# Attention in rounds of two pairs, with one PSUM ring of four bank pairs

## The chip, the core and the metric

The kernel runs on one core of a Trainium2 chip. The metric is the device time of one execution, in microseconds (us); the median of three runs is compared. All times below come from the runs of the kernel before and from one profiled execution of it.

## What is computed

Sigmoid attention over 8 batches of 12 heads (448 positions, head width 64), whose output, laid out as 3584 tokens by 768, goes through a feed-forward network with leaky ReLU:

```python
scores = scale * np.matmul(q, k.transpose(0, 1, 3, 2)) - np.log(S)
attn = 1.0 / (1.0 + np.exp(-scores))
attn_out = np.matmul(attn, v)
...
h = x @ w_in
out = np.maximum(0.01 * h, h) @ w_out
```

Everything arrives as fp32 except the two weight matrices, which are 64-bit floats and are turned into fp32 by integer operations on the chip.

## The kernel before

**Pairs.** Two heads make a pair, and there are 48 pairs; six pairs are one batch. For a pair the 448 keys are three chunks of 128 and a rest of 64. A *block* of scores is one chunk of one pair for both heads: six matmuls of form 64\*128 (64 rows of contraction, 128 columns of weights, 448 moving columns), since q and k are split into a high and a low part and three of the four products are summed, and since the two heads go side by side in the two halves of the rows. A block fills two PSUM banks, one per head. ScalarE turns it into a 128x896 tile `s` by one sigmoid (`attn`, line 414).

**Products with v** (`attn_v`, line 427) have the form 128\*64: two heads side by side in the two halves of the columns, six matmuls for the three chunks, accumulated in one bank (`pv`).

**Quarters.** The rest of 64 keys is done for two pairs at once, in the form 64\*64, where four matmuls go side by side: `last_scores` (line 419, eight matmuls on the unsplit q and k, one block of scores for two pairs) and, at the end of the odd pair's `attn_v(1)`, eight matmuls that add these chunks to the products of both pairs.

**Copies.** `keep` (line 442) copies a finished product (128x448) from PSUM into the tile `x` of its half batch. It is ScalarE that copies, for both pairs, in the slot after the odd pair's products are complete.

**PSUM.** Line 635 gives the scores three pairs of banks, used in turn (tag `s`), and the products two single banks (tag `pv`). Line 686 gives the feed-forward network six single banks, `px` and `pz`, once the attention's banks are closed.

**Order of the work.** The program order of every engine is written out: `slot` runs the chores that are due, then the work of the slot, and `later(n, ...)` files a chore n slots ahead. The main loop (lines 656 to 674) has four slots per pair j:

1. the third block of pair j (`scores(1)`);
2. the first two blocks of pair j + 1 (`scores(0)`);
3. pair j's v over chunks 0 and 1 (`attn_v(0)`);
4. chunk 2 (`attn_v(1)`), for an odd j the quarters with v, and then the quarter scores of the next two pairs.

For pair 0 the order differs: third block, quarter scores, v, and then the first two blocks of pair 1.

Filed beside them: the load of v two pairs ahead, the `high` of that pair (a cast of q and k, 128x832, on ScalarE; on VectorE where the plan of the slot puts an "h" item there) and its `low` (a subtraction on VectorE), and the load of q and k four pairs ahead.

**Other work in attention.** `PLAN_ATTN` (line 511) places operand work of the first feed-forward product: "h" items are ScalarE casts of 128x1344, "l" and "s" items VectorE subtractions and sums of 128x1344. `prepare(pace)` advances the weight preparation (`prep`, line 270) by 2.2 steps after every slot from j = 1 on: for each piece of 384 columns five VectorE operations and one load, for each unit four pieces, four sums, two stores and then seven empty steps (`WAIT`). `EARLY` (line 532) says in which slots near the end the first feed-forward weights are loaded and split (`advance`).

**After attention** come the feed-forward products, from `First.step` (line 562): the first one, `px_h`, starts directly after the last quarters with v.

Of the kernel before, what the change touches and what calls it, by code (L numbers as in the profile page):

```python
# [9 lines left out]
F32 = mybir.dt.float32  # L10
# [6 lines left out]
P = 128  # L17
# [7 lines left out]
ST = 10  # L25
AHEAD = 7

PACES = 2.2, 2
WAIT = 7
LATER = 4  # L30
IDLE = 7
# [20 lines left out]
def attn_ffn_kernel(ctx: ExitStack, tc: tile.TileContext, qk, v, w_in, w_out, out):  # L52
# [13 lines left out]
    S = qk.shape[3]  # L66
    NP = qk.shape[0] // B
    D = P // 2
    NK = 4
# [7 lines left out]
    heads = [slice(j * D, j * D + D) for j in range(2)]  # L77
# [5 lines left out]
    def pinned(issue):  # L83

        return lambda *args, **kw: tc.keep_in_program_order(issue(*args, **kw))  # L85

    mm, dma = pinned(nc.tensor.matmul), pinned(nc.sync.dma_start)
    copy, act, dma_act = (pinned(x) for x in (nc.scalar.copy, nc.scalar.activation, nc.scalar.dma_start))
    vcopy = pinned(nc.vector.tensor_copy)
# [14 lines left out]
    def later(slots, *fns, first=False):  # L104

        chores.setdefault(now + slots, ([], []))[not first].extend(fns)

    def slot(work=None):
        nonlocal now
        for fns in chores.pop(now, ()):  # L110
            for fn in fns:
                fn()
        if work is not None:
            work()
        now += 1
# [42 lines left out]
    class Quad:  # L158
# [14 lines left out]
        def take(self, what, acc, how=copy):  # L173
            t = self.pool.tile([P, S], F32, tag=self.tag, name=f"{what}_{self.name}", bufs=self.bufs)
            how(out=t, in_=acc[:, :S])
            return t
# [30 lines left out]
    ps = ExitStack()  # L207

    def banks(name, sizes, stack=ps):

        pool = stack.enter_context(tc.tile_pool(name=name, bufs=1, space=PSUM, reuse_waits="tile"))

        def psum(tag, name):
            bufs, n = sizes[tag]
            return pool.tile([P, n, 512] if n > 1 else [P, 512], F32, tag=tag, name=name, bufs=bufs)

        return psum
# [29 lines left out]
    def give(name):  # L247

        place = taken.pop(name)
        free[place[2]].append(place)  # L250
# [3 lines left out]
    attn = ExitStack()  # L254
    raws, spl, at = (attn.enter_context(tc.tile_pool(name=name, bufs=bufs, reuse_waits="tile")) for name, bufs in (
        ("raws", 4), ("spl", 2), ("at", 6)))
# [80 lines left out]
    xs = {}  # L337
# [10 lines left out]
    class Pair:  # L348
# [19 lines left out]
        def load_v(self):  # L368
            n = 2 * NK - 2 * (self.part == 1)
            t = ring.tile([P, 4 * HW], F32, tag="ring", name=f"v_{self.i}")  # L370
            self.v = t[:, :2 * NK * D].rearrange("p (a b) -> p a b", a=2 * NK)
            dma(out=self.v[:, :n], in_=v[self.i, :, :n])

        def high(self, how=None):
# [36 lines left out]
                    mm(**x[2])  # L411
                self.a.append(self.attn(c, ps))

        def attn(self, c, ps):
            s = at.tile([P, 2, S], F32, tag="s", name=f"s_{self.i}_{c}")
            act(out=s, in_=ps[:, :, :S], func=AF.Sigmoid, bias=bias, scale=scale)
            return s

        def last_scores(self):

            ps = psum("s", f"sc_{self.i}_{NK - 1}")
            for j, me in enumerate(heads):
                for y, rows in zip(pairs[self.i:], heads):
                    mm(ps[rows, j, :S], lhsT=y.raw[me, 1, S - D:], rhs=y.raw[me, 0], start=True, stop=True, skip_group_check=True)
            self.last = self.attn(NK - 1, ps)

        def attn_v(self, h):
            if h == 0:
                self.pv = psum("pv", f"pv_{self.i}")
            for c in range(2 * h, min(2 * h + 2, NK - 1)):  # L430
                for j, me in enumerate(heads):
                    mm(self.pv[me, :S], lhsT=self.v[:, (NK - 1) * j + c, :], rhs=self.a[c][:, j], start=c == 0, stop=False,
                       skip_group_check=True)
            if h == 1 and self.part == 2:
                x = pairs[self.i - 1]
                for j, me in enumerate(heads):
                    for y, rows in ((x, heads[0]), (self, heads[1])):
                        mm(y.pv[me, :S], lhsT=self.v[rows, 2 * NK - 2 + j, :], rhs=x.last[rows, j],
                           start=False, stop=True, skip_group_check=True)
                later(1, x.keep, self.keep, first=True)  # L440

        def keep(self):
            half, c = divmod(self.i, NB)
            if c == 0:
                xs[half] = take(f"x_{half}", F32, SIDES[half % 2 and half > KEPT])
            copy(out=xs[half][:, c], in_=self.pv[:, :S])
            if half >= KEPT and c == NB - 1:
                dma(out=xd[half - KEPT], in_=xs[half])
                give(f"x_{half}")

    class Operands:
# [57 lines left out]


    PLAN_ATTN = {
        "e13.1": "h002", "e15.1": "l002", "e17.1": "h102", "e19.1": "l102", "e20.1": "s302", "e22.1": "s202", "e24.1": "s402",
        "e26.1": "s102", "e27.1": "h402", "e29.1": "l402", "e30.1": "h502", "e32.1": "l502", "e33.1": "h302", "e35.1": "l302"}
    COMMON = {
        "p12": "h002", "p13": "l002", "p15": "s302", "p19": "h102", "p20": "l102", "p23": "s202", "p27": "s402", "p36": "s102",
        "p33": "h402"}
# [12 lines left out]
                w1.append((NOP * (p * NU + u) + ORDER.index(members[0]), Weights(0, u, g, ring, "ring")))  # L529


    EARLY = {(-4, 0): -8, (-4, 2): -6, (-3, 0): -4, (-2, 0): -3, (-1, 0): -2, (-1, 2): -1, (0, 0): 0}
    at_load, at_high, at_low = 0, 0, 0
    w1_stage = [stage] * 3

# [80 lines left out]
    last = B * NP - 1  # L616
    pairs = [Pair(i) for i in range(B * NP)]
# [14 lines left out]
    pairs[1].low()  # L632
    pairs[3].load_qk()
    ops = [Operands(q) for q in range(NQ)]
    psum = banks("ps_a", dict(s=(3, 2), pv=(2, 1)))

    def go(todo, work, pace=0):


        for x, what in todo:  # L640
            for y in what.split():
                later(0, lambda x=x, y=y: x.do(y))
        slot(work)
        prepare(pace)

    def ending(j):

        pairs[j].attn_v(1)
        if j % 2 and j < last:
            pairs[j + 1].last_scores()  # L650

    unread = psum("s", "unread")[:, 0]
    for _ in range(IDLE):
        mm(unread[heads[0], :S // 4], lhsT=zeros[:, :D], rhs=zeros, start=True, stop=True)
    slot(lambda: pairs[0].scores(0))
    for j in range(last + 1):
        works = [lambda: pairs[j].scores(1)] + [lambda: pairs[j + 1].scores(0)] * (j < last)
        works += [lambda: pairs[j].attn_v(0), lambda: ending(j)]
        if j == 0:

            works = [works[0], pairs[0].last_scores, *works[2:], works[1]]
        if j + 2 <= last:
            later(0, pairs[j + 2].load_v)

            later(1, lambda j=j: pairs[j + 2].high(vcopy if PLAN_ATTN.get(f"e{j}.1", "").startswith("h") else copy))
            later(2, pairs[j + 2].low)
        if j + 4 <= last:
            later(4, pairs[j + 4].load_qk)
        for n, work in enumerate(works):
            go([(ops[0], PLAN_ATTN.get(f"e{j}.{n}", ""))], work, PACES[0] * (j > 0))  # L670

            t = EARLY.get((j - last, n))
            if t is not None:
                advance(t)

    kept, chores[now] = chores[now][0], ([], chores[now][1])
# [9 lines left out]
    psum = banks("ps_f", dict(px=(3, 1), pz=(3, 1)))  # L686
    size = NU * NOP

    def product(q, first, k):
        todo = []  # L690
        for x, key in ((q, f"np{k}"), (q + 1, f"p{k}")):
            if x < NQ:
                todo.append((ops[x], PLANS[x].get(key, "")))
        go(todo, first.step, PACES[1] * (7 <= k < size - 7 and k % 7 in (6, 0, 1, 2)))

    for q in range(NQ - 1):
        first = First(q, ops[q])
# [5 lines left out]
    first = First(NQ - 1, ops[-1])  # L703
# [7 lines left out]
    more = ExitStack()  # L711
# [26 lines left out]
    for k in range(NOP, size):  # L738
        m, at = divmod(k - NOP, 6)
        if m < AHEAD:  # L740
            x = w2[use[m]]
# [22 lines left out]
    for i, (g, u) in enumerate(use[AHEAD:]):  # L764
        one = len(GROUPS[g]) == 1
        pool, tag = (ring, "ring") if i < len(GROUPS) else (t2b, "t1" if one else "t2")
        w2[g, u] = Weights(1, u, g, pool, tag, NU if one else None)
    psum = banks("ps_o", dict(px=(3, 1), pz=(5, 1)))
# [12 lines left out]
    for k, (p, n, u0) in enumerate(items):  # L781
# [5 lines left out]
        ending = k == len(items) - 1  # L787

        def work():
            for i, step in ((k, "load"), (k - 1, "high"), (k - 2, "low")):  # L790
                if 0 <= i < len(use) - AHEAD:
                    getattr(w2[use[AHEAD + i]], step)()
            g_load(k + 3)
            g_high(k + 2)
            g_low(k + 2)
            x = gs.pop(k)[1]
            for m, (acc, begins) in enumerate(accs):
                for e in range(KS):
                    u = u0 + e
                    parts_mm(acc, w2[g, u].of(n), slice(m * P, m * P + P), x[:, 0, e], x[:, 1, e], begins and u == 0, u == NU - 1)  # L800
                if ending and m < NB - 1:
                    store(p, m, quads[m].done(n))
                elif ending:

                    t = op.tile([P, S], F32, tag="o", name="end", bufs=8)
                    b = 2 * p
                    for cols, how, queue in zip(HALVES, (copy, vcopy), (dma, dma_act)):
                        how(out=t[:, cols], in_=acc[:, cols])
                        queue(out=out[NB + m, :, b * S + cols.start:b * S + cols.stop], in_=t[:, cols])
# [46 lines left out]
```

## Time and profile before

| | |
|---|---|
| median of 3 runs | 1070.38 us (1070.28 to 1072.77) |
| span of the profiled execution | 1070.4 us |
| attention, from the first score to the first feed-forward matmul | 4.02 to 260.18 us |
| granted TensorE clock, mean | 1.000 |
| attention, 20 to 250 us: ScalarE's sigmoids | 152 of 0.935 us |
| VectorE, 21 to 52 us | busy 21.33 of 31.00 us |
| VectorE, 147 to 179 us | busy 26.73 of 32.00 us |

PE stands for TensorE, PEld for its weight loads, ACT for ScalarE, DVE for VectorE, SP for the engine that issues most DMAs. In a row such as `PE MATMUL pv<-s,v 128*64`, the tile left of the arrow is written from those right of it, with the rows and columns of the weights after it. `sc` is a block of scores, `pv` a product with v, `s` a sigmoid's output, `qk` the raw q and k of a pair and `qks` their split parts, `x` the attention output in SBUF; `wr`, `wd`, `ws`, `t` belong to the weight preparation, `px_h` and `py_h` to the feed-forward network. All operations are recorded through one helper, so every row says L85 and they are told apart by tiles. A row of a group gives the busy time and the mean of one in ns, then the idle time of the engine before them and what ended it.

### The profile page before, as it was taken

The numbers are of one execution on the slowest core, as the hardware profiler recorded it, in microseconds if no ns is written. First come the engines' busy times: TensorE is split into PE (matmuls) and PEld (weight loads), VectorE is DVE, ScalarE is ACT, GpSimd is POOL, SyncE is SP. The second block draws the span as 40 slices with busy tenths as digits, with TensorE's granted clock in tenths as the row PEclk, the third lists the DMA queues.
The fourth block names the chain that finished last, engine by engine and source line by source line (L and its number), as shares of the span: only waits on it lengthen the run. The fifth ranks groups of instructions, "written<-read, shape, count | busy, mean of one in ns | idle before, by whom it ended". The sixth has DMA issues, their size and how long they took to land.

```text
span 1070.4 us, 16070 instructions
## 1 busy us (share of the span) xinstructions
PE 1065.7 (100%) x5882; PEld 885.5 (83%) x5882; DVE 672.6 (63%) x1021; ACT 581.9 (54%) x833; POOL 0.3 (0%) x5
## 2 busy tenths in 40 slices
PE   9999999999999999999999999999999999999998
PEld 5454444445999999999999999999999999999997
DVE  4767878676797898878977666655332423333332
ACT  6787878777554655566555555554333233323331
POOL 0000000000000000000000000000000000000000
PEclk9999999999999999999999999999999999999999
DMA  7787688788899789999898887877544545455552
GB/s 246 246 298 273 240 286 297 259 304 310 246 292 313 211 280 318 278 293 342 252 316 266 268 260 247 323 260 215 183 154 126 184 147 164 121 185 151 151 159 86
DMA packets 107935, 255.61 MB, mean 239 GB/s; under 512 B 11984, under 2 KB 55888, under 8 KB 107856
## 3 DMA queue, kind: packets, MB, share of 16 engines
q1 hardware_dynamic: 107280, 254.02, 72.6%
q8 instruction: 46, 0.75, 0.3%
q10 hardware_dynamic: 576, 0.57, 0.2%
q14 instruction: 33, 0.27, 0.1%
HBM read 167.38 MB, written 87.16 MB: 238 GB/s over the span
## 4 chain that ended last, share of the span: by engine, by line
PE 99%; ACT 0%; ACTq 0%; DVE 0%; issue 0%
PE px_h L85 22%; PE px_o L85 22%; PE pv L85 13%; PE sc L85 11%; PE pz_o L85 11%; PE pz_h L85 11%; PE py_o L85 5%; PE py_h L85 5%; ACTq L85 0%; ACT L85 0%; DVE end L85 0%; ACT end L85 0%; ACT qks L85 0%; ACT warm L85 0%
## 5 line engine op out<-in xcount | busy, mean ns | idle before, releaser
L85 DVE TENSOR_TENSOR gs<-gg,gs 128x896 fp32r<-128x896 f32 x112 | 122.4, 1093 | 226.8 <-ACT gs L85 226.8
L85 PE MATMUL px_o<-gs,w 128*128 128x448 f32 x1152 | 232.5, 362 | 0.0
L85 PE MATMUL px_h<-hi,w 128*128 128x448 f32 x768 | 231.7, 362 | 0.0
L85 PEld LDWEIGHTS px_o<-gs,w 128*128 128x128 f32 x1152 | 216.0, 188 | 14.4
L85 ACT CAST gs<-gg 128x896 fp32r<-128x896 f32 x112 | 105.5, 943 | 220.4 <-PE px_o L85 117.6
L85 ACT ACTIVATE s<-sc 128x896 f32<-128x896 f32 x168 | 150.4, 934 | 45.8 <-PE sc L85 45.7
L85 PEld LDWEIGHTS px_h<-hi,w 128*128 128x128 f32 x768 | 144.0, 187 | 10.7 <-issue 0.7
L85 PE MATMUL pv<-s,v 128*64 128x448 f32 (+1 forms) x768 | 140.9, 551 | 0.0
L85 PE MATMUL px_h<-lo,w 128*128 128x448 f32 x384 | 138.9, 362 | 0.0
L85 DVE TENSOR_TENSOR w<-wx,w 128x768 fp32r<-128x768 f32 (+1 forms) x160 | 136.0, 852 | 3.3 <-ACT w L85 2.8
L85 ACT CAST w<-wx 128x768 fp32r<-128x768 f32 (+1 forms) x160 | 119.6, 751 | 7.2 <-DMA wx<-t 7.1
L85 PE MATMUL pz_h<-hi,w 128*128 128x448 f32 x384 | 118.3, 362 | 0.0
L85 PE MATMUL pz_o<-gs,w 128*128 128x448 f32 x576 | 116.5, 362 | 0.0
L85 PEld LDWEIGHTS pz_o<-gs,w 128*128 128x128 f32 x576 | 108.0, 188 | 7.2
L85 PEld LDWEIGHTS sc<-qks 64*128 64x128 f32 x876 | 77.6, 189 | 40.8 <-issue 31.0
L85 PEld LDWEIGHTS pv<-s,v 128*64 128x64 f32 (+1 forms) x768 | 42.1, 135 | 77.2 <-issue 68.3
L85 PE MATMUL sc<-qks 64*128 64x448 f32 (+1 forms) x876 | 103.0, 377 | 0.1
L85 DVE TENSOR_TENSOR qks<-qk,qks 128x832 fp32r<-128x832 f32 (+3 forms) x51 | 49.5, 973 | 57.2 <-ACT qks L85 55.8
L85 ACT COPY c_h<-px_h 128x448 f32<-128x448 f32 x64 | 34.2, 534 | 90.8 <-PE px_h L85 87.6
L85 PEld LDWEIGHTS pz_h<-hi,w 128*128 128x128 f32 x384 | 72.0, 188 | 5.0
L85 PEld LDWEIGHTS px_h<-lo,w 128*128 128x128 f32 x384 | 72.0, 187 | 4.4
L85 DVE SCALAR_TENSOR_TENSOR wd<-wr,wd 128x384 int32<-128x384 int32 x128 | 71.3, 557 | 3.3
(51 smaller groups left out, 952.9 us busy)
## 6 DMA issues: line engine op xcount, KB each, us to landing
gg<-g SPq DMA_DIRECT2D x112, 448.0 KB, 3.5
wx<-t SPq DMA_DIRECT2D x120, 384.0 KB, 4.4
g<-c_h SPq DMA_DIRECT2D x128, 224.0 KB, 4.5
g<-s SPq DMA_DIRECT2D x96, 224.0 KB, 4.4
qk<-in_qk SPq DMA_DIRECT2D x46, 448.0 KB, 5.7
wr<-in_w_in SPq DMA_DIRECT2D x32, 384.0 KB, 3.7
t<-ws SPq DMA_DIRECT2D x16, 768.0 KB, 6.9
wr<-in_w_out SPq DMA_DIRECT2D x32, 384.0 KB, 4.2
```

Source lines behind the costliest of these rows:

```text
L85: return lambda *args, **kw: tc.keep_in_program_order(issue(*args, **kw))
```

## The change

The loop goes by 24 rounds of two pairs, x and y, in five slots:

Slot 0: all three blocks of x. Slot 1: all three blocks of y. Slot 2: x with v, all three chunks. Slot 3: y with v. Slot 4, `ending`: the quarter scores of the next two pairs first, then the quarters with v of this round (`last_v`, split off from `attn_v`).

In round 0 the order is: x with v (its scores and quarter scores went ahead), the blocks of y, an empty slot, y with v, `ending`.

The products of both pairs of a round share one tile `both` of two banks, taken from the same ring as the scores; the ring has four bank pairs and is all of PSUM. Eight requests are made per round: six blocks, `both`, the quarter scores. The copy of x's product stays on ScalarE, that of y goes to VectorE (`vcopy`), both at the beginning of the next slot.

The quarter scores' sigmoid is written into a free part of the odd pair's v tile (`room`), so that the six buffers of tag `s` serve the six blocks alone.

Beside them: the v loads of the next two pairs in slots 0 and 1, the high of the even one of them in slot 2, its low and the odd one's high in slot 3, the odd one's low in slot 4; the q and k loads of the two pairs after those in slots 1 and 4. The preparation's paces are 4, 5, 4.2, 2.8 and 2 steps for the five slots, from round 1 on. The plan's items and `EARLY` are given by round and slot.

```diff
-PACES = 2.2, 2
+PACES = (4, 5, 4.2, 2.8, 2), 2
...
-            self.last = self.attn(NK - 1, ps)
+            self.last = self.attn(NK - 1, ps, pairs[self.i + 1].room)
...
+        def attn_v(self):
+            mate = pairs[self.i - 1]
+            if self.part == 1:
+                self.both = psum("s", f"pv_{self.i}")
+            self.pv = (self if self.part == 1 else mate).both[:, self.part - 1]
+            for c in range(NK - 1):
...
+        def last_v(self):
+
+            x = pairs[self.i - 1]
+            for j, me in enumerate(heads):
+                for y, rows in ((x, heads[0]), (self, heads[1])):
+                    mm(y.pv[me, :S], lhsT=self.v[rows, 2 * NK - 2 + j, :], rhs=x.last[rows, j],
+                       start=False, stop=True, skip_group_check=True)
+            later(1, x.keep, lambda: self.keep(vcopy), first=True)
...
+        (6, 3): "h002", (7, 1): "l002", (8, 3): "h102", (9, 1): "l102", (10, 1): "s302", (11, 1): "s202", (12, 1): "s402",
+        (13, 1): "s102", (13, 3): "h402", (14, 1): "l402", (15, 3): "h502", (16, 1): "l502", (16, 3): "h302", (17, 1): "l302"}
...
+    EARLY = {(-1, 0): (-8,), (-1, 2): (-6,), (-1, 4): (-4,), (0, 2): (-3,), (0, 3): (-2, -1), (0, 4): (0,)}
...
-    psum = banks("ps_a", dict(s=(3, 2), pv=(2, 1)))
+    psum = banks("ps_a", dict(s=(4, 2)))
...
+    def whole(x):
+        x.scores(0)
+        x.scores(1)
+
+    def ending(x, y):
+
+        if y is not None:
+            y.last_scores()
+        x.last_v()
...
     slot(lambda: pairs[0].scores(0))
+    slot(lambda: pairs[0].scores(1))
+    slot(pairs[0].last_scores)
+    rounds = (last + 1) // 2
+    for r in range(rounds):
+        x, y, *more = pairs[2 * r:2 * r + 6]
+        works = [lambda: whole(x), lambda: whole(y), x.attn_v, y.attn_v, lambda: ending(y, more[0] if more else None)]
+        if r == 0:
+
+            works = [works[2], works[1], lambda: None, *works[3:]]
+        if more:
+            z, w = more[:2]
+            how = vcopy if PLAN_ATTN.get((r, 3), "").startswith("h") else copy
+            later(0, z.load_v)
+            later(1, w.load_v)
+            later(2, z.high)
+            later(3, z.low, lambda: w.high(how))
+            later(4, w.low)
+        for n, far in enumerate(more[2:]):
+            later(1 + 3 * n, far.load_qk)
         for n, work in enumerate(works):
+            go([(ops[0], PLAN_ATTN.get((r, n), ""))], work, PACES[0][n] * (r > 0))
+            for t in EARLY.get((r - rounds + 1, n), ()):
                 advance(t)
```

More of the change, by code (lines that the diff above doesn't have):

```diff
@@ L371, in load_v @@
             self.v = t[:, :2 * NK * D].rearrange("p (a b) -> p a b", a=2 * NK)
+            self.room = t[:, 2 * NK * D:2 * NK * D + 2 * S].rearrange("p (a b) -> p a b", a=2)
             dma(out=self.v[:, :n], in_=v[self.i, :, :n])
@@ L412, in scores, with attn @@
                 self.a.append(self.attn(c, ps))
-        def attn(self, c, ps):
-            s = at.tile([P, 2, S], F32, tag="s", name=f"s_{self.i}_{c}")
+        def attn(self, c, ps, s=None):
+            if s is None:
+                s = at.tile([P, 2, S], F32, tag="s", name=f"s_{self.i}_{c}")
             act(out=s, in_=ps[:, :, :S], func=AF.Sigmoid, bias=bias, scale=scale)
@@ L424, in last_scores @@
                     mm(ps[rows, j, :S], lhsT=y.raw[me, 1, S - D:], rhs=y.raw[me, 0], start=True, stop=True, skip_group_check=True)
-            self.last = self.attn(NK - 1, ps)
[L427 to L430, printed above, removed]
+            self.last = self.attn(NK - 1, ps, pairs[self.i + 1].room)
[5 more added lines that the diff above has]
+            for c in range(NK - 1):
                 for j, me in enumerate(heads):
@@ L433, in attn_v, with keep @@
                        skip_group_check=True)
[L434 to L442, printed above, removed]
+        def last_v(self):
[5 more added lines that the diff above has]
+            later(1, x.keep, lambda: self.keep(vcopy), first=True)
+        def keep(self, how=copy):
             half, c = divmod(self.i, NB)
@@ L445, in keep @@
                 xs[half] = take(f"x_{half}", F32, SIDES[half % 2 and half > KEPT])
-            copy(out=xs[half][:, c], in_=self.pv[:, :S])
+            how(out=xs[half][:, c], in_=self.pv[:, :S])
             if half >= KEPT and c == NB - 1:
@@ L511, in attn_ffn_kernel @@
     PLAN_ATTN = {
-        "e13.1": "h002", "e15.1": "l002", "e17.1": "h102", "e19.1": "l102", "e20.1": "s302", "e22.1": "s202", "e24.1": "s402",
-        "e26.1": "s102", "e27.1": "h402", "e29.1": "l402", "e30.1": "h502", "e32.1": "l502", "e33.1": "h302", "e35.1": "l302"}
+        (6, 3): "h002", (7, 1): "l002", (8, 3): "h102", (9, 1): "l102", (10, 1): "s302", (11, 1): "s202", (12, 1): "s402",
+        (13, 1): "s102", (13, 3): "h402", (14, 1): "l402", (15, 3): "h502", (16, 1): "l502", (16, 3): "h302", (17, 1): "l302"}
     COMMON = {
@@ L529, in attn_ffn_kernel @@
                 w1.append((NOP * (p * NU + u) + ORDER.index(members[0]), Weights(0, u, g, ring, "ring")))
-    EARLY = {(-4, 0): -8, (-4, 2): -6, (-3, 0): -4, (-2, 0): -3, (-1, 0): -2, (-1, 2): -1, (0, 0): 0}
+    EARLY = {(-1, 0): (-8,), (-1, 2): (-6,), (-1, 4): (-4,), (0, 2): (-3,), (0, 3): (-2, -1), (0, 4): (0,)}
     at_load, at_high, at_low = 0, 0, 0
@@ L644, in go @@
         prepare(pace)
[L646 to L650, printed above, removed]
+    def whole(x):
[5 more added lines that the diff above has]
+        x.last_v()
     unread = psum("s", "unread")[:, 0]
@@ L655, in attn_ffn_kernel @@
     slot(lambda: pairs[0].scores(0))
[L656 to L668, printed above, removed]
+    slot(lambda: pairs[0].scores(1))
[16 more added lines that the diff above has]
+            later(1 + 3 * n, far.load_qk)
         for n, work in enumerate(works):
-            go([(ops[0], PLAN_ATTN.get(f"e{j}.{n}", ""))], work, PACES[0] * (j > 0))
-            t = EARLY.get((j - last, n))
-            if t is not None:
+            go([(ops[0], PLAN_ATTN.get((r, n), ""))], work, PACES[0][n] * (r > 0))
+            for t in EARLY.get((r - rounds + 1, n), ()):
                 advance(t)
```

## The prediction

> **What bounds the kernel now.** I read the page first: busy shares, then the chain that ended last.
>
> ```profile
> PE 1065.7 (100%) x5882; PEld 885.5 (83%) x5882; DVE 672.6 (63%) x1021; ACT 581.9 (54%) x833; POOL 0.3 (0%) x5
> ...
> PE 99%; ACT 0%; ACTq 0%; DVE 0%; issue 0%
> ```
>
> TensorE (PE) is the chain from end to end; a saved microsecond of PE is a saved microsecond of the kernel as long as nothing else becomes late. The profiled execution spans 1070.4 us, which is also the median of the runs, so I count against 1070.4. Next the chain in order of time inside attention: start, length, what, matmuls. Two pairs make four pieces. Matmuls run two at a time here (x18 is nine couples), the quarters four at a time.
>
> ```profile
> 219.91 2.02 PE sc L85 x18
> 221.93 2.40 PE pv L85 x12
> 224.34 2.02 PE sc L85 x18
> 226.36 3.32 PE pv L85 x20
> 229.68 2.77 PE sc L85 x26
> 232.44 2.41 PE pv L85 x12
> ```
>
> From 224.34 to the same place two pairs later is 2.02 + 3.32 + 2.77 + 2.41 = 10.52 us. PE never waits long inside, yet the pieces are longer than their matmuls. To see that, I take the pitch of each form away from a change of form:
>
> ```profile
> 203.53 1.58 PE L85 MATMUL sc<-qks 64*128 64x448 f32 x14
> ```
>
> ```profile
> L85 PE MATMUL px_h<-hi,w 128*128 128x448 f32 x152 | 46.0, 362 | 0.0
> ```
>
> ```profile
> 203.22 1.72 PEld L85 LDWEIGHTS sc<-qks 64*128 64x128 f32 x18 [0.70 <-issue]
> ...
> 254.01 0.14 PEld L85 LDWEIGHTS pv<-s,v 128*64 128x64 f32 x2 [0.23 <-issue]
> ...
> 255.14 0.14 PEld L85 LDWEIGHTS pv<-s,v 128*64 128x64 f32 x2 [0.23 <-issue]
> ```
>
> Fourteen score matmuls (seven couples) take 1.58; less the 0.36 that one lasts, six steps of 0.203. The loads for products with v go 254.01, 254.38, 254.76, 255.14: steps of 0.377. Nine score couples are then 1.83 of a 2.02 piece (0.19 over), six couples with v 2.26 of 2.41 (0.15 over). The excess sits at the edges, where the form goes from 64\*128 (scores) to 128\*64 (v): the weight load there idles 0.70 "<-issue" (first row of the last fence), which names no other engine.
>
> **The changes of form.** Before, two pairs have: scores to v (twice), v to scores (once), v to quarters, quarters to scores. After: scores to v, v to quarters, quarters to scores, once each. Removed per round is one whole short visit: a pv x12 and a sc x18 piece lose their excess as they join their neighbours, 0.15 + 0.19 = 0.34 us; that is one pair of edges, each piece's excess being its beginning and its end. Matmuls, sigmoids, casts, loads: same numbers. Round 0 keeps its old order (v of pair 0 straight after its scores), so 23 of the 24 rounds gain: 23 x 0.34 = **-7.8 us**; a round becomes 10.52 - 0.34 = 10.18.
>
> The Trainium skill (TensorEngine Tiling (Array Packing), Key Properties) says that changing the tiling mode drains TensorE while changing only the tile does not; with the constant of about 166 ns of a warm lone matmul (TensorE: Matmul & The Clock Gate, Single matmul latency) two drains would be an estimated 0.33 a round, 7.6 us in all. The trace's edges agree at 0.34, with the excess on those edges alone.
>
> **Start and end.** Before, round 0 already scores two blocks of pair 2, late because their operands were late:
>
> ```profile
> 12.41 3.50 PE sc L85 x30
> ...
> 250.70 2.95 PE sc L85 x26
> 253.65 2.41 PE pv L85 x12
> 256.06 0.81 PE sc L85 x5
> 256.86 3.32 PE pv L85 x20
> 260.18 2.00 PE px_h L85 x9
> ```
>
> ```profile
> 260.23 0.97 ACT L85 COPY x<-pv 128x448 f32<-128x448 f32 x2 [2.35 <-PE pv L85]
> ```
>
> Fifteen couples at 0.203 and 0.19 of edges make 3.24, against 3.50: **-0.3**, as those blocks now come a round later. Near the end the x26 piece took 2.95 against 2.77 (scores waited for the ring of three): **-0.2**. Against this: the ring of four now fills all eight banks, and it is used in turn: five requests before round 0 (unread, three blocks and the quarters of pair 0), five in round 0, then eight in each round with the products as the seventh. So from round 1 on the products with v are the 17th, 25th, ... request, so they always get the first bank pair. The first FFN product (px_h) takes the first bank, which before belonged to scores long read. Now it must wait for the copy out of that bank: last matmul, then a copy as at 260.23 (two in 0.97, 0.54 for one), where px_h now begins at 260.18. That is 0.05 + 0.54 + a hand-over of 0.1, so up to 0.7; 0 if the new pool's banks lie otherwise. I take **+0.6**.
>
> **What the longer runs ask of ACT and DVE.** Now a score block needs the bank pair that was requested four requests earlier to be read. Time t runs from a round's first score.
>
> ```profile
> L85 ACT ACTIVATE s<-sc 128x896 f32<-128x896 f32 x152 | 136.4, 935 | 41.2 <-PE sc L85 41.2
> L85 ACT CAST qks<-qk 128x832 fp32r<-128x832 f32 x39 | 35.0, 896 | 6.1 <-DMA qk<-in_qk 6.1
> L85 ACT COPY x<-pv 128x448 f32<-128x448 f32 x44 | 21.2, 539 | 0.0
> ```
>
> ```profile
> 253.43 2.58 ACT L85 ACTIVATE s<-sc 128x896 f32<-128x896 f32 x3
> ```
>
> ACT: three sigmoids in a row take 2.58, so one per 0.82. PE scores a block in 0.61 (three couples) with 0.1 of edge on the first. The first block's last matmul ends at t = 0.87; sigmoids end at 1.9, 2.7, 3.5, 4.4, 5.2, 6.0. Blocks five and six need sigmoids one and two at t = 2.5 and 3.1; the products with v need the third at 3.75. All ready, the last by 0.2. The mate's v begins at 6.1 with the fourth (4.4) and needs the sixth (6.0) at 7.6. ACT's copy of the first product comes before these sigmoids and ends by 0.7. Its sum a round, 7 x 0.82 + 2 x 0.8 + 0.5 = 7.8, fits in 10.18. The cast of the next pair (its "high") follows the sixth sigmoid and ends at t = 6.8. A 1.3 us "h" cast of the plan then still leaves ACT free at 8.9, before the quarter's sigmoid at 9.6. No stall from ACT.
>
> DVE is different: the mate's copy is new work for it, and block three of the next round waits for it.
>
> ```profile
> L85 DVE TENSOR_TENSOR c_h<-c_h,py_h 128x448 f32<-128x448 f32 x7 | 4.3, 620 | 4.1 <-PE py_h L85 4.0
> ...
> L85 DVE CAST qks<-qk 128x832 fp32r<-128x832 f32 x5 | 2.9, 589 | 0.9 <-DMA qk<-in_qk 0.9
> ```
>
> ```profile
> L85 DVE SCALAR_TENSOR_TENSOR wd<-wr,wd 128x384 int32<-128x384 int32 x87 | 48.5, 558 | 2.5
> L85 DVE TENSOR_TENSOR qks<-qk,qks 128x832 fp32r<-128x832 f32 x43 | 44.0, 1024 | 50.3 <-ACT qks L85 50.3
> L85 DVE TENSOR_SCALAR wd<-wd 128x384 f32<-128x384 f32 x43 | 15.5, 360 | 1.3
> ...
> L85 DVE TENSOR_TENSOR ws<-wd,ws 128x384 f32<-128x384 f32 x22 | 12.2, 555 | 0.4
> ...
> L85 DVE TENSOR_TENSOR lo<-x,hi 128x1344 fp32r<-128x1344 f32 x4 | 6.2, 1551 | 0.0
> ```
>
> No row has DVE copying a product. The nearest reads a product of 448 columns in 0.62; by its cast between SBUF tiles (832 columns in 0.59) it would be 0.32. I take 0.62, the row with the same source. The Trainium skill (VectorE: DVE Perf Modes, Why PSUM operands drop a tier) also holds that an fp32 operand in PSUM loses the doubled rate that SBUF copies can have; no run here shows the copy alone yet.
>
> The weight preparation: six steps of a piece are three ops of 0.36 and two of 0.56, 2.2 us; a unit is four pieces, four sums of 0.55 and seven empty steps, 11 us in 35 steps, 0.31 a step, or 0.365 while no step is empty. The paces give 18 steps a round (17.6 before): 5.6 us on average. With two "lows" of 1.02 and the copy, 8.3 of 10.18: no bound on average. But the order counts. Copy from 0.1 to 0.7; slots 0 to 2 hold 13.2 steps, 4.8, to 5.5; the first low waits for ACT's high (6.8), to 7.8; 2.8 steps, to 8.9; second low, to 9.9; 2 steps, to 10.6. The next copy should begin at 10.3, so it begins 0.3 late and ends at 11.2; block three starts at 10.18 + 0.71 + 0.61 = 11.5. About 0.2 is spare. The work of slots 3 and 4 cannot move ahead of the high, so lateness there is not made good by DVE's idle time before it.
>
> Nine rounds (7, 9 to 14, 16, 17) have one more DVE op of 1.55 in slot 1: DVE is free at 7.1 instead of 5.5, 0.3 after the high. That is 0.1 beyond the spare, and nothing if the empty steps fall there. Five rounds (6, 8, 13, 15, 16) do the second pair's high on DVE (0.59) in slot 3: 0.4 beyond. Rounds 13 and 16 have both, 0.7. Lateness carries into the next round, where an l or s op follows each time: for the seven rounds with that op alone I put 0.5 together, though 0.1 is beyond the spare in each. Three times 0.4, two times 0.7, and the 0.5: 3.1 as the upper working, 0 if empty steps and the overlap of neighbouring DVE ops cover all of it. Before, no bank waited for DVE, so nothing of this showed. I take **+2.5**, nearer the worked end.
>
> The sum: 1070.4 - 7.8 - 0.3 - 0.2 + 0.6 + 2.5 = **1065.2 us**.
>
> The loads: the far pairs' q and k go out in slot 1 and slot 4, the casts come in slots 2 and 3 of the next round; ACT waited for them six times before (6.1 in all), and has 2 us spare there now. Price 0, unless they are late as below. FFN is untouched and starts earlier with its weights prepared.
>
> **Rivals.**
>
> *No DVE stall.* The copy is nearer 0.32, or the empty steps fall well. Then only edges and ends remain: 1070.4 - 7.8 - 0.5 + 0.6 = 1062.7, as low as 1062.0 if px_h does not wait. For it: DVE idles 50 us behind ACT's highs in the view above. Against: that idle time lies ahead of the high. Chance 0.27.
>
> *Slower: the ring closes a loop over three engines.* Block three of a round, four sigmoids, the high, low, steps, low, steps, copy, block three again: 0.7 + 3.3 + 0.9 + 1.0 + 1.0 + 1.0 + 0.7 + 0.6 and hand-overs of 0.5 make 9.7. Its place is the high, if q and k land late each time behind the queue of weight loads, which itself waits for DVE:
>
> ```profile
> ACT qks L85 <- DMA qk<-in_qk: 6.1, 6, 1.9
> ...
> DVE wd L85 <- DMA t<-wd: 2.5, 3, 1.1
> ```
>
> From 0.5 late on each round the loop sets the pace; from 0.84 the round is longer than 10.52 and the kernel slower. With 1.1 late a round is 10.8, 0.28 more than before; 23 of them and the ends make about 1077. The six waits before, of 1.0 in the mean, in 23 rounds speak against it. Chance 0.06.
>
> *The edges are not form but hand-over.* If the 0.34 is the wait for another engine's sigmoid or copy, it stays as the v products still begin on fresh sigmoids: 1070.4 - 0.5 + 0.6 + 2.5 = 1073. Against: block follows block at 0.203 though each waits for a bank. Chance 0.03.
>
> *Half the gain lost.* As forecast, but the lateness of DVE runs through twice as many rounds (5.5 instead of 2.5): 1068.2. Chance 0.12. The forecast has the remaining 0.52.
>
> **How the numbers follow.** A difference of 0.3%, 3.2 us, is what the measurement can tell; so "faster" is below 1067.2. The forecast (mostly 1063.7 to 1066.5) and the rival without a stall lie there, with a part of the half-lost case: 0.85. Same: most of the half-lost case, 0.08. Slower: the loop and the hand-over's tail, 0.07. The range takes in no stall and no px_h wait at the bottom, 1062.0, and the half-lost case at the top, 1068.2.
>
> **What would show it.** Right: chain pieces of 36 score matmuls in about 3.75 us and 24 with v with no piece between; a steady round of 10.2; the weight load's 0.70 gaps three to a round; the stalls only at block three, in rounds 6 to 17, released by DVE's copy; a gap of 0.7 ahead of px_h released by a copy. Wrong: rounds of 10.2 everywhere (copy cheaper), stalls in rounds without plan items (loop), or edges of the old size inside the long runs.

## The result, and the profile after

| | before | after |
|---|---|---|
| median | 1070.33 us (1070.1 to 1072.77, 4 runs) | 1063.05 us (1062.42 to 1063.37, 4 runs) |
| ratio | | 0.9927, interval 0.9915 to 0.9940 |
| span of the profiled execution | 1070.4 us | 1061.3 us |

The change saves 7.3 us. The prediction said 1065.2, in the range 1062.0 to 1068.2. Its largest term holds; three smaller ones don't, and they partly cancel.

An execution takes about 1.8 us more than its span (1063.13 against 1061.3 in the profiled one of after), and some executions, of the kernel before and of variants of the changed one, start at half pace for some microseconds and are about 2 us longer; the profiled one of before is such an execution, so its span of 1070.4 stands beside the median of 1070.33 by accident.

TensorE's run of one round after, from the timeline (start, length, engine, operation, matmuls); a stretch is merged while its group stays the same:

```profile
107.65 3.91 PE L85 MATMUL sc<-qks 64*128 64x448 f32 x36
111.49 4.73 PE L85 MATMUL pv<-s,v 128*64 128x448 f32 x24
116.15 0.98 PE L85 MATMUL sc<-qk 64*64 64x448 f32 x8
```

Six blocks in one run, both pairs with v in one run, then quarters: three edges. From the first score at 107.65 to that of the next round is 10.17 us, 0.35 less than 10.52. The run with v goes from x to y at 0.376 as it does inside a pair: a new bank and fresh sigmoids, but no new form, and no excess.

Where the 9.0 us between the two spans (1070.36 and 1061.34) went, on the profile's own clock:

| stretch | before | after | difference |
|---|---|---|---|
| to pair 2's scores (before: to its third block, less 1.21 for the two early blocks) | 18.71 | 16.05 | -2.7 |
| 22 rounds, to the last round's first score | 231.46 | 224.17 | -7.3 |
| last round, to px_h (before with those 1.21) | 9.94 | 9.41 | -0.5 |
| feed-forward part and end | 810.25 | 811.71 | +1.5 |

Of the first line 2.3 belongs to the half-pace start of before's execution: two runs below that have the changed start at half pace reach pair 2 at 18.39 and 18.40. The rows of both starts:

```profile
4.02 4.18 PE L85 MATMUL sc<-qks 64*128 64x224 f32 x30
8.12 1.77 PE L85 MATMUL sc<-qk 64*64 64x448 f32 x8
...
19.92 1.28 PE L85 MATMUL sc<-qks 64*128 64x448 f32 x10
```

```profile
4.00 2.54 PE L85 MATMUL sc<-qks 64*128 64x224 f32 x30
6.47 1.13 PE L85 MATMUL sc<-qk 64*64 64x448 f32 x8
...
16.05 1.28 PE L85 MATMUL sc<-qks 64*128 64x448 f32 x10
```

The same 30 matmuls take 4.18 in one and 2.54 in the other. The clock record in the traces goes with it: its first entry at full speed begins at 10.10 us in before and at 4.40 in after. The mean of 1.000 in the table ahead of the prediction counts the time without an entry as full speed. Over all runs that entry begins between 4.3 and 6.3 us in seven traces and between 10.0 and 10.5 in five; where it falls among the first scores, their pitch goes from 0.213 a couple to 0.11 at that place.

The views that answer to the prediction's steps, after: first what weight loads waited for in attention (total, times, longest), then the same from the end of attention to 700 us, then the start of the feed-forward part.

```profile
PEld pv L85 <- issue: 63.7, 273, 0.7
PEld sc L85 <- issue: 31.0, 44, 0.7
PEld pv L85 <- ACT s L85: 6.5, 22, 0.3
PEld sc L85 <- DVE x L85: 0.8, 3, 0.3
```

```profile
PEld px_h L85 <- DVE w L85: 1.6, 2, 1.2
```

```profile
248.72 0.98 PE L85 MATMUL pv<-v 64*64 64x448 f32 x8
249.63 0.48 PE L85 MATMUL px_h<-hi,w 128*128 128x448 f32 x1
```

Scores wait for DVE's copy in three rounds only, 0.5 us together by the round times. The 0.3 ahead of a round's first products with v, which the view puts down to a sigmoid, is no stall: that load idles the same 0.30 in before (at 205.25, with no engine named). px_h begins 0.48 after the last four quarter matmuls begin (0.49 in before): no wait for a copy. But the feed-forward part, which had no gap before, has two: its matmuls come 1.0 late at 497 us and 0.2 at 396, each with another 0.1 behind it.

### The profile page after: what moved, and what is told of

Read it like the earlier page. It is cut to its first block, busy times and chain, and to the rows that moved or that the text cites. A ratio compares the mean times of both kernels' runs of the same rounds, so it can differ in the third digit from the quotient of the medians.

```text
span 1061.3 us, 16140 instructions
## 1 busy us (share of the span) xinstructions
PE 1055.8 (99%) x5882; PEld 889.0 (84%) x5882; DVE 684.2 (64%) x1045; ACT 569.9 (54%) x809; POOL 0.3 (0%) x5
## 4 chain that ended last, share of the span: by engine, by line
PE 53%; DVE 0%; ACT 0%; issue 0%
PE px_o L85 22%; PE pz_o L85 11%; PE px_h L85 8%; PE py_o L85 5%; PE pz_h L85 4%; PE py_h L85 2%; DVE end L85 0%; ACT end L85 0%
## 5 line engine op out<-in xcount | busy, mean ns | idle before, releaser
L85 ACT ACTIVATE s<-sc 128x896 f32<-128x896 f32 x144 | 119.4, 933 | 8.8 <-PE sc L85 8.8
L85 PE MATMUL pv<-s,v 128*64 128x448 f32 x576 | 113.8, 543 | 0.0
L85 PE MATMUL sc<-qks 64*128 64x448 f32 (+1 forms) x876 | 95.1, 367 | 0.1
L85 PEld LDWEIGHTS pv<-s,v 128*64 128x64 f32 x576 | 39.1, 137 | 63.3 <-issue 54.1
L85 PE MATMUL pz_h<-lo,w 128*128 128x448 f32 x192 | 69.6, 363 | 0.0
```

## The experiments

Times are medians, ratios against the kernel of before on the same chip (1070.34 to 1070.64 there). After is 1063.05, 0.9927. Round times are read from the first scores of neighbouring rounds.

**The old visits with the new banks.**

```diff
+        if r:
+            works[1] = lambda: y.scores(0)
+            works[3] = lambda: (y.scores(1), y.attn_v())
```

> The changed kernel, but from round 1 on the third block of y is scored between x's v and y's v, so that a round again has the visits of before (five blocks, x with v, one block, y with v, quarters); ring, copies and all else as changed. Theory (the edge between forms costs): 0.35 a round, 23 rounds, about 1071, steady rounds of 10.52. Rival (the gain came from the ring of four banks or the copies, and edges cost nothing by themselves): about 1063, rounds of 10.17.

1077.81 (1077.13 to 1078.38), ratio 1.0067 (1.0050 to 1.0084). One of the short rounds, and then the last piece with v of a long one with the load inside it:

```profile
92.87 3.30 PE L85 MATMUL sc<-qks 64*128 64x448 f32 x30
96.09 2.48 PE L85 MATMUL pv<-s,v 128*64 128x448 f32 x12
98.50 0.86 PE L85 MATMUL sc<-qks 64*128 64x448 f32 x6
99.29 2.52 PE L85 MATMUL pv<-s,v 128*64 128x448 f32 x12
```

```profile
109.84 2.84 PE L85 MATMUL pv<-s,v 128*64 128x448 f32 x12
```

```profile
111.70 0.20 PEld L85 LDWEIGHTS pv<-s,v 128*64 128x64 f32 x4 [0.92 <-ACT s L85]
```

Four rounds took 10.55, one 10.54 and most of the others 10.86 to 10.89. The short ones are nearly the edges alone, 0.38 over 10.17. The long ones wait 0.33 more, ahead of the mate's last chunk with v, for that chunk's sigmoid: in this order ScalarE takes the highs of the next pairs first. The five short rounds are 6, 8, 13, 15 and 16, just those in which the plan gives the second high to VectorE. So ring and copies of the change, with the visits of before, give nothing back; the order of the matmuls is the gain. The time itself is 6.7 beyond the expectation, most of it by that sigmoid.

**Edges with no hand-over.**

```diff
+        if r and more:
+            works[1] = lambda: (more[0].last_scores(), whole(y))
+            works[4] = lambda: ending(y, None)
...
-            later(1 + 3 * n, far.load_qk)
+            later(n, far.load_qk)
```

> The changed kernel, but the quarter scores of the next round stand between the blocks of x and those of y (q and k of the far pairs are loaded one slot each earlier or later for it, slots 0 and 1 instead of 1 and 4). This adds one edge 64*128 to 64*64 and one back, with operands that were ready long before, so no hand-over of fresh data. Theory (an edge costs whoever hands over): 0.36 a round more, rounds of 10.53, about 1071. Rival (the cost of an edge is the hand-over of a sigmoid): rounds of 10.17 to 10.25, about 1063 to 1065.

1072.62 (1070.40 to 1073.86), ratio 1.0015 (1.0005 to 1.0024).

```profile
102.92 2.09 PE L85 MATMUL sc<-qks 64*128 64x448 f32 x18
104.94 0.98 PE L85 MATMUL sc<-qk 64*64 64x448 f32 x8
105.86 2.08 PE L85 MATMUL sc<-qks 64*128 64x448 f32 x18
```

20 of 22 rounds take 10.52: 0.35 more for one edge out and one back, with q and k that lay in SBUF for many microseconds. (One round lost a further 1.4, behind a late copy on DVE.) This run's view puts the idle time ahead of y's blocks down to a sigmoid:

```profile
105.86 1.71 PEld L85 LDWEIGHTS sc<-qks 64*128 64x128 f32 x18 [0.70 <-ACT s L85]
```

That sigmoid had ended 0.2 before, at 105.64, and the idle 0.70 is what the load of scores shows at its edge with no engine named. So the edge costs, not the wait for a sigmoid; the rival of the hand-over is out.

**The ring of three.**

```diff
-    psum = banks("ps_a", dict(s=(4, 2)))
+    psum = banks("ps_a", dict(s=(3, 2), both=(1, 2)))
```

> The changed kernel with the banks of before: three pairs for the scores, one pair of its own for the products. Same order of matmuls. Theory (six blocks in a row run ahead of ScalarE's one sigmoid per 0.82, so the fourth pair is needed): blocks four to six wait for sigmoids one to three, v begins about 0.45 later, rounds of about 10.6, 1073. Rival (the ring size does not matter, the order alone does): 1063.

1074.71 (1074.37 to 1075.05), ratio 1.0038 (1.0023 to 1.0053); rounds of 10.69 to 10.71, one of 10.79.

```profile
102.28 1.72 PEld L85 LDWEIGHTS sc<-qks 64*128 64x128 f32 x18 [0.70 <-issue]
104.23 0.50 PEld L85 LDWEIGHTS sc<-qks 64*128 64x128 f32 x6 [0.23 <-ACT s L85]
105.04 0.50 PEld L85 LDWEIGHTS sc<-qks 64*128 64x128 f32 x6 [0.31 <-ACT s L85]
105.85 0.50 PEld L85 LDWEIGHTS sc<-qks 64*128 64x128 f32 x6 [0.31 <-ACT s L85]
106.66 0.20 PEld L85 LDWEIGHTS pv<-s,v 128*64 128x64 f32 x4 [0.30 <-DVE wd L85]
```

Blocks four to six come 0.81 apart, ScalarE's pace, where the three blocks ahead of them took 1.95 with the edge. The six blocks run in a row without waits only with the fourth bank pair in the ring: without it the edges' 0.35 are paid back as 0.53.

**The kernel of before again.** No edit.

> The kernel of before, one more look, for the first 20 us. The profiled execution of before had its first scores at half pace (224 columns at 0.207 a couple until 6.9 us, the first quarters at 0.8 to 0.9) and that of the changed kernel full pace from 4.6 us. If the slow start belongs to the kernel of before: span 1070.4 again. If it belongs to that one execution: a span near 1068, 2 us shorter, and round times of 10.52 all the same.

1072.65, span 1070.9, rounds of 10.51 to 10.56: a second execution with the half-pace start (its first score of pair 2's third block comes as late as in the first). 13 executions of before on that chip fall into nine from 1070.04 to 1071.00 and four from 1071.88 to 1072.27, none between. Their spans are 1068.2 to 1069.2 and 1070.1 to 1070.5, and the two traced spans, 1070.4 and 1070.9, lie in the second group and just above it. I read that group as the half-pace starts, and the median as without; no profile of before with the other start is at hand, so this is argued from the two groups, not shown.

**Copies on ScalarE.**

```diff
-            later(1, x.keep, lambda: self.keep(vcopy), first=True)
+            later(1, x.keep, self.keep, first=True)
```

> The changed kernel, but ScalarE copies both products, as before. Theory (DVE's copy of y, late in rounds 7, 14 and 18, holds up the fourth block): those three stalls, 0.5 us together, are gone, every round is 10.17, about 1062.5. Rival (the stalls come from the mate's low and not from the copy): the stalls stay. Second rival (ScalarE, with 0.43 more, falls behind its six sigmoids): rounds longer than 10.17 everywhere, up to 0.43 each, 1073.

1062.49 (1062.34 to 1064.46), ratio 0.9927 (0.9914 to 0.9940). All rounds 10.17 but one of 10.22: the three stalls were DVE's copy. ScalarE has room for the second one. Against after it is within the measurement.

**The preparation at its old step.**

```diff
-PACES = (4, 5, 4.2, 2.8, 2), 2
+PACES = (4, 5, 4.2, 2.8, 1.875), 2
```

> The changed kernel with 1.875 instead of 2 steps of weight preparation in slot 4: 412 steps are done in attention, as before the change, instead of 415, so that the preparation stands at the same step when the feed-forward part begins. Theory (the feed-forward part lost 1.45 us in the changed kernel because the preparation's VectorE operations now fall ahead of the sums and lows of weights there): no gaps in the feed-forward part, 1061.6. Rival (the gaps come from the earlier start, from transfers or from the order in which banks were left): the gaps of 1.2 and 0.4 stay, 1063.

1066.80 (1065.24 to 1069.23), ratio 0.9960 (0.9946 to 0.9974). The feed-forward part has no gap any more: the theory on its 1.45 us holds. From px_h to the end takes 810.2 in every trace with 412 steps (both of before and the three changed ones), and 810.6 to 811.7 in the seven with 415; what sets the size among the seven was not tried. But four rounds of attention take 11.04, 11.74, 10.39 and 11.91, 4.4 us together:

```profile
PEld sc L85 <- DVE x L85: 4.7, 4, 1.7
```

An eighth of a step less per round shifts the seven empty steps of the preparation against the rounds, and DVE's copy then begins up to 2.9 us after the round's first score, as it stands in DVE's program order behind the next pairs' lows and the preparation. This is the forecast's stall, and larger than forecast. In the feed-forward part of after, the same shift puts two preparation operations ahead of a chain that ends in the low of a weight tile:

```profile
493.50 1.15 DVE L85 SCALAR_TENSOR_TENSOR wd<-wr,wd 128x384 int32<-128x384 int32 x2
494.57 0.61 DVE L85 TENSOR_TENSOR c_h<-c_h,py_h 128x448 f32<-128x448 f32 x1
495.10 0.62 DVE L85 TENSOR_TENSOR s<-s,c_h 128x448 f32<-128x448 f32 x1
495.63 1.55 DVE L85 TENSOR_TENSOR s<-x,x 128x1344 f32<-128x1344 f32 x1
497.10 0.95 DVE L85 TENSOR_TENSOR w<-wx,w 128x768 fp32r<-128x768 f32 x1
```

px_h's weight load at 498.11 waits for that last row. Before, the last four rows stand in the same order, with an idle 1.3 ahead of them in place of the first.

**Both edits.** Copies on ScalarE and 1.875.

> The two edits before together: copies on ScalarE and 412 steps. If both theories hold the gains add: 0.5 and 1.45, about 1061.1.

1063.17 (1062.66 to 1063.43), ratio 0.9925 (0.9913 to 0.9938). No gap in the feed-forward part, but one round of 11.17 in which scores wait twice for lows (1.1 together). The gains do not add: with the copy gone, what DVE is late with is the low.

**The copy twice.**

```diff
             how(out=xs[half][:, c], in_=self.pv[:, :S])
+            if how is vcopy:
+                how(out=xs[half][:, c], in_=self.pv[:, :S])
```

> The changed kernel with VectorE copying y's product twice, the second copy over the first. Theory (the fourth block waits for the copy, which in a quiet round ends some 0.45 before that block starts): 0.62 more makes the fourth block wait about 0.2 in every round and 0.6 in the three late ones, and with VectorE's heavier queue some more rounds are late: rounds of 10.3 to 10.4, 1067 to 1069. What the prediction had (the third block waits): 0.6 more of slack would be missing, rounds of 10.9, 1080. Rival (no block waits for this copy): 1063.

1076.89 (1075.57 to 1078.11), ratio 1.0054 (1.0040 to 1.0069). Quiet rounds take 10.53, and six rounds longer still, up to 11.73. The two copies of a quiet round whose first score is at 59.46, and the load of its fourth block:

```profile
60.22 1.28 DVE L85 COPY x<-pv 128x448 f32<-128x448 f32 x2 [0.63 <-ACT x L85]
```

```profile
61.62 1.54 PEld L85 LDWEIGHTS sc<-qks 64*128 64x128 f32 x16 [0.44 <-ACT s L85]
```

Counted from the round's first score, the third block begins on time, at 1.32, before even the first copy has ended (1.38); the fourth begins at 2.19 instead of 1.93, behind the second copy (2.04). So it is the fourth block that waits. Its row names a sigmoid, but that had ended at 61.36, before the second copy did at 61.50. The copy ends 0.66 later than in a quiet round of after and the block begins 0.26 later, which leaves 0.40 to spare, close to the 0.45 that I had read. The dose is right in sign and too small in size: a quiet round loses 0.36, since the block behind the fourth loses a little too, and the late rounds lose more than the 0.6 expected.

**A bank pair for each product.**

```diff
-            mate = pairs[self.i - 1]
-            if self.part == 1:
-                self.both = psum("s", f"pv_{self.i}")
-            self.pv = (self if self.part == 1 else mate).both[:, self.part - 1]
+            self.pv = psum("s", f"pv_{self.i}")[:, self.part - 1]
```

> The changed kernel, but y's product has a bank pair of its own from the ring (nine requests a round) instead of the other half of the tile it shares with x's. In the changed kernel VectorE's copy of y began 0.03 after the end of ScalarE's copy of x in every round in which VectorE was free. Theory (it waits for it because both read one tile): here the copy begins with ScalarE's, 0.5 earlier in quiet rounds; quiet rounds stay at 10.17, the three late rounds stay late, as there VectorE itself is late, so 1063 again, within 1. Rival (it waits since both write one tile x, or since the two engines are kept apart otherwise): the copy stays behind ScalarE's.

1063.29 (1062.40 to 1064.37), ratio 0.9927 (0.9910 to 0.9944). The copies in the timeline, ScalarE's and DVE's of round 1 here, then of round 1 of after:

```profile
18.58 0.53 ACT L85 COPY x<-pv 128x448 f32<-128x448 f32 x1
```

```profile
18.55 0.62 DVE L85 COPY x<-pv 128x448 f32<-128x448 f32 x1
```

```profile
16.25 0.53 ACT L85 COPY x<-pv 128x448 f32<-128x448 f32 x1
```

```profile
16.80 0.62 DVE L85 COPY x<-pv 128x448 f32<-128x448 f32 x1 [0.66 <-ACT x L85]
```

Here DVE starts beside ScalarE's copy, or while it runs, wherever it is free in time; in after it waits for it, and never started less than 0.03 after ScalarE's end, in any of the 24 rounds, whether the two x tiles were the same or not. The shared tile `both` is what orders them. One round is late, by 0.13, instead of three. This execution had the half-pace start and reaches pair 2 at 18.39, against 18.71 before: the change itself saves 0.3 at the start.

**Steps moved ahead of the high.**

```diff
-PACES = (4, 5, 4.2, 2.8, 2), 2
+PACES = (6, 6, 4.875, 1, 0), 2
```

> The changed kernel with 17.875 steps of preparation a round (412 in all, as before the change and as in the run with the pace of before), but as 6, 6, 4.875, 1 and 0 in the five slots. Theory (the lateness of the copy is VectorE work queued behind the next pair's high, while VectorE idles ahead of it): the late rounds of the run with the pace of before, 4.4 us together, shrink to 1 or less, and the feed-forward part has no gaps: 1061.5 to 1062.5. Rival (the total of VectorE's work in the full rounds makes it late, wherever it stands): the 4.4 stay, 1066.8.

1065.19 (1063.14 to 1066.42), ratio 0.9946 (0.9932 to 0.9959). No gaps in the feed-forward part, 2.7 us of late rounds (up to 11.29) instead of 4.4. Neither theory gets its number. DVE now waits elsewhere, for the store of a decoded weight tile:

```profile
DVE wd L85 <- DMA t<-wd: 12.8, 5, 3.5
```

Steps that come in a burst reach the buffer whose store to HBM is still under way (this wait was 6.0 in the run with the old step). That these waits make the rounds late is argued from the view, not tried by itself. No version beat the changed kernel by more than the measurement can tell.

## Why the prediction was right, and where it was not

**The edges: right.** 0.34 a round was forecast, 10.18 for a round; measured 0.35 and 10.17, 19 of 22 rounds. The rule of the Trainium skill (TensorEngine Tiling (Array Packing), Key Properties), that a change of mode drains and a change of tile does not, agrees: the step from x to y inside the run with v costs nothing, the inserted quarters cost 0.35. One row was misplaced: the load that idles 0.70 is that of scores or quarters behind v, and the load from scores to v idles 0.30, so a round has two gaps of 0.70 (44 for scores in the view of after) and not three. The sum took the excess from the pieces and is not touched by this.

**ScalarE keeps up: right**, and by little, as said: the ring of three shows the blocks at its 0.81, and the ring of four none.

**Start and end: right** in size (0.3 by the run with two tiles, which starts as slowly as before; the last round 0.53 shorter, of which 0.35 is the edge).

**The base: not seen.** I took the equality of span and median for a fact about the kernel. It hid two things of about 2 us that cancel, the time outside the span and the half-pace start. Since the sum was of differences, the forecast lost nothing by it, but against the span alone the kernel would have seemed to gain 9.0.

**px_h's wait, 0.6: wrong; the failing step is "it is used in turn".** Banks are not handed out in the order of requests. The listing could have refuted the count: taken in turn, the tenth request, the quarter scores of round 0, falls on the pair of the sixth, `both`, which is not read before PE has done the quarters with v behind those scores; the program would have stopped there, and it runs. In the program as built, the third block waits for ScalarE (by the order of issue for the quarter block's sigmoid, ahead of the copies) and the fourth for DVE's copy. The pair that was given back first in the program is taken first, so the count "17th, 25th" means nothing, and the first bank was free for px_h. That px_h has no wait is measured; that the order of giving back is the rule fits these waits and was not tried by itself.

**DVE's stall, 2.5: the mechanism right, the size not;** 0.5 was measured, in rounds 7, 14 and 18, behind three of the rounds named (6, 13 and 17). Two steps were off. Block three does not wait but block four, 0.61 later. And the copy does not begin at 0.1 but at 0.76, behind ScalarE's, since they share a tile. A quiet round has 0.4 to spare where I had 0.2, and DVE may come to the copy some 0.5 later than I had worked out before it shows: begun at 1.07 it cost nothing (round 8), at 1.23 it cost 0.10 (round 7). The size also hangs on where the empty steps fall: 0.5 here, 4.4 with an eighth of a step less a round, nothing without the copy. I had written that clause, and took the worked end; the chance of no stall should have been larger. (A slip beside it: 0.365 a step is that of a piece, 2.2 in six steps; with the sums a unit is 11 us in 28 steps, 0.39.)

**"FFN is untouched": wrong**, and 1.45 us in the traced execution (0.3 to 1.45 over the seven traces with 415 steps). The paces sum to 18 steps a round instead of 17.6, so the preparation enters the feed-forward part three steps further on (415 instead of 412), and its VectorE work falls on a stretch that had no room. The step was there to be taken: I counted the steps for DVE's load in attention and not for what follows.

The sum as measured, on equal starts: 23 edges -8.1, stalls +0.5, start -0.3, end -0.2, feed-forward +1.5: -6.6 of the 7.3. The rest, 0.7, is not accounted for; the medians come from other executions than the traces, and the feed-forward part alone differs by up to 1.1 between runs with equal steps.

That the time lies in the range is in part luck. The two terms taken too large, 0.6 and 2.0, and the one put at nothing, 1.45, partly cancel: without the last, the traced execution would have taken about 1061.7, below the bottom of 1062.0 (1062.1 by its own terms). The measured time is nearer the rival without a stall, 1062.7, than the forecast.

## What to carry to other kernels

Where TensorE is the bound, count the changes of matmul form and what each costs, from pieces of the chain against the pitch inside them: grouping equal forms pays, until the longer run asks more buffers than there are. When an operation moves to an engine that also works through a background list, the list's phase decides the cost, not its average; look for the places where both meet, also behind the part that was changed. A bank ring's order and what shares a tile are read from the waits of the built program; a count from the source is followed through the whole program order, where this one would have stopped in round 0.

## What the hardware showed that I had not expected

Two copies out of different banks of one tile, by different engines, ran one after the other (0.03 between end and start in every quiet round) and side by side from two tiles (from 18.58 and 18.55 in the rows above); the ordering is the program's, and the engines can read PSUM at the same time.

DVE copied 448 fp32 columns out of PSUM in 0.62, as the subtraction from PSUM did; ScalarE in 0.53. The Trainium skill (VectorE: DVE Perf Modes, Why PSUM operands drop a tier) holds that an fp32 operand in PSUM keeps DVE at its single rate. The trace agrees: DVE's cast between SBUF tiles takes 0.59 for 832 columns, nearly twice as many.

The start at half pace (30 matmuls in 4.18 instead of 2.54) is of the kind that the Trainium skill (TensorE: Matmul & The Clock Gate, Part 1: The HAM clock gate) describes: a cold array at half rate, let go by a free-running window, at a point that varies from run to run. The traces agree on the half pace and show the clock record turning to full speed with it. They differ in the spread, which the section gives as half a microsecond either way: here the turn comes between 4.3 and 10.5 us, with the first matmul at 1.03 in every trace. What lets it go early in some executions was not tried, and stays open.
